# A new instruction order from batch 6 on, output passes exchanged, and the last store cut into quarters

## The chip, the core and the metric

The kernel runs on one core of a Trainium2 chip. Its five engines each take their own instructions in order and wait for one another by semaphores: TensorE (PE in the profile), VectorE (DVE), ScalarE (ACT), GpSimd (POOL) and SyncE (SP, which here only issues DMA transfers). The metric is device time in microseconds (us), lower is better.

## The reference

Two parts are chained. First an attention with pooled keys and values, for 8 batches, 8 heads, 576 positions of 64 channels, in fp32; then a feed-forward layer on the 4608 resulting rows.

```python
k_p = k.reshape(B, H, S // 8, 8, D).mean(axis=3)      # 72 pooled keys per head
v_p = v.reshape(B, H, S // 8, 8, D).mean(axis=3)
attn = softmax(q @ k_p.T / sqrt(D))
x = (attn @ v_p).transpose(0, 2, 1, 3).reshape(4608, 512)
h = x @ w_in                                          # 512 -> 2048
out = (h * sigmoid(1.702 * h)) @ w_out                # 2048 -> 512
```

## The kernel before

The result has to be exact to fp32 while the matmuls run in the fast fp32r mode, so each operand is split into a high and a low part and each product is three matmuls (high by high, high by low, low by high). From batch 2 on the products with w_in are combined by a scheme with seven block products for eight; for the last 512 rows ("late", called batch 7 here) w_out is treated the same way. Weight blocks in their combined form lie in DRAM and are fetched again for each batch.

The stretch that matters here, from about 650 us on, has four parts:

- Batch 6. For each of eight pairs p of feature tiles: products `ha6_p`, `hb6_p` (hidden units), activation, products `o6_*` (output, accumulated over the pairs in four PSUM banks). At its end ScalarE copies each `o` bank to an `osb` tile and issues its store at once (`finish`).
- The late hidden products (`hidden`): per pair seven products `la`, `lb`, `lc` of six 128x512 matmuls. Their operands are the combined weights `ws7_p` (three loads of 512 KB and one of 256 KB per pair, on SP's queue), their results are kept, added and passed through the activation by ScalarE and VectorE into tiles `store{p}_{th}`. PSUM banks are reused within a pair, so the next product waits for the copy of the last.
- Beside it `fold_out` combines the blocks of w_out: for each pair sums `u`, then high and low parts `tf{p}_0`, `tf{p}_1`, `tf{p}_2`, which SP stores to DRAM (`td{p}`) and later loads again (`ta{p}`, `tb{p}`). `tf{p}_2` takes its memory from the same two tiles as `osb`, so such a tile is free only when the store that reads it has landed.
- Two output passes (`outgoing`), th = 0 and th = 1, one per half of the late columns: for each of eight pairs seven products `m1` to `m7` of six 128x256 matmuls into seven PSUM banks, whose operands (`oa`, `ob`, `oc`, `od`, and sums `ou`) ScalarE, VectorE and GpSimd cut from `store`. At the end of a pass `combined` adds the seven banks into output tiles, which are stored: th = 0 goes to 512 rows in one piece (two transfers of 512 KB), th = 1 to the last 64 rows of each batch (four of 256 KB).

The order of all instructions is written out in the string `ORDER`, which a planner made beforehand; the kernel only reads it. A token is an engine and a task: `P:la7_4#1` is the second task of that name on TensorE; A is ScalarE, V VectorE, G GpSimd, D a transfer issued by SP, O a store of results. A star says that the task runs on its other engine, VectorE. Each engine gets its tasks in the order of the string. The costs that `plan.add` is given (0.7 for a store, say) were the planner's; when the kernel is built they have no effect. For `finish` the store is issued with the copy (`A:osb...`), and its `O` token emits nothing.

Of the kernel before, what the change touches and what calls it, by code (L numbers as in the profile page):

```python
# [14 lines left out]
ALU = mybir.AluOpType  # L15
# [3 lines left out]
P = 128  # L19
# [371 lines left out]
A:ah7_1#1 A:xtl0_0#3 V:al7_1#1 G:gl6_5#3 P:o6_128#10 *G:gl6_5#1 A:cs6_6#3 D:ws6_6#3 P:pav7_1#0 V:mt7_1#2 P:o6_384#10
P:o6_0#11 P:ha6_6#3 P:o6_128#11 A:xtl1_0#0 D:ws7_0#1 *A:ah7_1#2 P:pav7_1#1 A:yt1_0#0 A:cs6_6#4 A:gh6_6#1 P:ha6_7#0
V:cs6_6#1 A:gh6_6#0 P:hb6_6#2 P:o6_384#11 *A:y1_0#2 A:cs6_7#0 G:yt1_0#0 *A:xtl1_1#0 G:xtl0_1#0 *A:y1_1#2 V:al7_1#2
V:mt7_1#3 *A:xtl1_1#1 A:cs6_6#5 A:cs6_6#2 A:xtl1_0#1 P:ha6_7#1 P:o6_256#11 A:yt3_1#0 A:yt1_1#0 V:y1_1#2 A:cs6_7#1
V:cs6_6#2 *G:xtl1_0#0 A:gh6_6#3 V:y1_0#2 A:ah7_1#3 A:gh6_6#2 D:ws7_0#0 P:hb6_7#0 P:hb6_7#1 A:cs6_6#6 G:gl6_6#0
P:ha6_7#2 *G:gl6_6#1 G:yt1_1#0 V:al7_1#3 A:yt3_0#0 A:y2_1#0 P:pav7_1#3 *G:yt3_0#0 *A:y1_1#3 *G:yt3_1#0 A:cs6_7#3
P:pav7_1#2 A:cs6_6#7 A:xtl1_0#2 P:ha6_7#3 A:xtl1_1#3 P:o6_128#12 D:ws7_0#2 V:y1_1#3 A:y1_0#3 *G:y2_1#0 V:cs6_7#1
A:y2_0#0 D:ws7_1#0 V:y1_0#3 *G:gl6_6#3 V:cs6_7#0 *G:gl6_6#2 P:o6_0#12 A:xtl1_1#2 *G:xtl1_1#0 A:y2_1#1 *G:y2_0#0
P:o6_0#13 P:lb7_1#0 *G:xtl0_2#0 A:gh6_7#0 A:cs6_7#4 A:yt2_0#0 A:cs6_7#2 A:yt1_1#1 P:o6_384#12 P:hb6_7#2 *A:y2_0#1
*G:gl6_7#0 P:o6_256#12 G:xtl0_0#1 A:gh6_7#2 P:o6_128#13 A:yt4_1#0 P:o6_384#13 A:gh6_7#1 *G:y2_1#1 A:cs6_7#6  # L400
*G:gl6_7#2 D:ws7_1#3 *G:yt2_0#0 P:la7_0#0 P:o6_256#13 A:yt3_1#1 V:cs6_7#2 A:yt2_1#0 *G:y2_0#1 A:cs6_7#5 A:xtl1_0#3
*G:xtl1_1#1 A:gh6_7#3 P:la7_1#0 D:ws7_1#2 A:cs6_7#7 *G:yt2_1#0 A:yt4_0#0 G:yt4_1#0 *G:yt1_1#1 A:yt2_1#1 A:yt3_0#1
# [99 lines left out]
class Plan:  # L502
# [6 lines left out]
    def add(self, engine, us, emit, reads=(), writes=(), due=None, table=None, also=(), port=False, other=None, mode=None, lag=2.2):  # L509


        t = Task()
# [28 lines left out]
        for b in also:  # L541
            if b not in t.bufs:
                t.bufs.append(b)
                b.users += 1
# [31 lines left out]
def attention_moe_kernel(ctx: ExitStack, tc: tile.TileContext, q, k, v, w_in, w_out, out):  # L576


    nc = tc.nc
# [1910 lines left out]
```

## Time and profile before

| | us |
|---|---|
| median of 3 runs | 893.15 (892.63 to 893.85) |
| profiled execution | 894.48 |
| span of its profile, first to last instruction | 892.7 |
| TensorE busy | 872.2 |
| VectorE, ScalarE, GpSimd busy | 698.4, 538.0, 343.6 |
| mean granted TensorE clock | 0.992 |

The profiled execution has 1.8 us outside the span. Matmuls are pipelined and their ends are modelled, so TensorE counts as busy from the start of a matmul to the modelled end of the last; a gap in it is a wait, and its cost is read there and not from the share of the span.

### The profile page before, as it was taken

Reading aid. Unit: us, or ns where it says so; the run is one execution under the profiler, and the core shown is the slowest. Engines: PE = TensorE matmul, PEld = TensorE weight load, DVE = VectorE, ACT = ScalarE, POOL = GpSimd, SP = SyncE. Lnnn points to the kernel's source line nnn. Section 1 sums busy time; section 2 is a strip of 40 time slices with the busy share of each in tenths; the row PEclk is TensorE's granted clock in tenths of the full one; section 3 lists DMA queues with packets and bytes.
Section 4 is the critical chain, followed back from the end, with each engine's and each line's share of the span. In section 5 each row is a group of like instructions: output and inputs, shape, how many; then the busy total and the mean of one; then the engine's idle time right before and its main releaser. Section 6 shows DMA issues by size and latency. Waiting matters only on the chain.

```text
span 892.7 us, 15828 instructions
## 1 busy us (share of the span) xinstructions
PE 872.2 (98%) x5404; PEld 781.6 (88%) x5404; DVE 698.4 (78%) x1376; ACT 538.0 (60%) x1186; POOL 343.6 (38%) x345
## 2 busy tenths in 40 slices
PE   7999999999999999999999999999999999799997
PEld 6889898878899999998999989989998987589997
DVE  6998998779887876788878877889778756568885
ACT  4987655466556765767666665685657643247531
POOL 2768646666222124222521252236311226233322
PEclk9999999999999999999999999999999999899999
DMA  9972635646585768757884768567764448685011
GB/s 269 381 231 65 196 69 194 204 170 189 174 278 161 229 229 249 224 168 215 240 234 150 229 190 250 182 194 241 216 207 157 159 153 292 206 291 225 2 48 48
DMA packets 145792, 174.33 MB, mean 195 GB/s; under 512 B 85168, under 2 KB 96432, under 8 KB 145712
## 3 DMA queue, kind: packets, MB, share of 16 engines
q1 hardware_dynamic: 141392, 165.45, 59.4%
q10 hardware_dynamic: 4320, 7.87, 2.3%
q8 instruction: 43, 0.70, 0.3%
q14 instruction: 37, 0.30, 0.1%
HBM read 141.95 MB, written 31.33 MB: 194 GB/s over the span
## 4 chain that ended last, share of the span: by engine, by line
PE 87%; DMA 3%; DVE 3%; ACT 2%; SPq 1%; issue 1%; POOL 1%; DVEq 0%; POOLq 0%; ACTq 0%
PE ha L1881 13%; PE hb L1881 10%; PE m L2376 9%; PE o L2085 8%; PE o L2086 8%; PE o L2087 8%; PE sps L1127 4%; PE la L2154 3%; PE h L1676 3%; PE h L1677 3%; PE h L1678 3%; PE o L1718 2%; PE o L1719 2%; PE o L1720 2%; PE lc L2154 2%
## 5 line engine op out<-in xcount | busy, mean ns | idle before, releaser
L1935 POOL TENSOR_TENSOR glall<-shared,ghall 128x256 fp32r<-128x256 f32 x76 | 60.0, 794 | 203.4 <-ACT shared L1928 149.9
L2085 PE MATMUL o<-w,ghall 128*128 128x512 f32 x320 | 126.9, 397 | 0.0
L2086 PE MATMUL o<-w,ghall 128*128 128x512 f32 x320 | 126.2, 394 | 0.0
L2087 PE MATMUL o<-w,glall 128*128 128x512 f32 x320 | 125.0, 391 | 0.0
L2087 PEld LDWEIGHTS o<-w,glall 128*128 128x128 f32 x320 | 60.1, 188 | 13.8 <-POOL glall L1935 0.3
L1881 PE MATMUL ha<-xs,ws 128*128 128x256 f32 x480 | 71.1, 284 | 0.0
L1881 PEld LDWEIGHTS ha<-xs,ws 128*128 128x128 f32 x480 | 65.8, 190 | 4.8 <-ACT shared L1896 1.0
L1881 PE MATMUL hb<-x,ws 128*128 128x256 f32 x480 | 67.3, 283 | 0.0
L1881 PEld LDWEIGHTS hb<-x,ws 128*128 128x128 f32 x480 | 63.7, 190 | 3.0 <-DVE shared L1903 0.2
L2085 PEld LDWEIGHTS o<-w,ghall 128*128 128x128 f32 x320 | 60.6, 189 | 6.2
L2086 PEld LDWEIGHTS o<-w,ghall 128*128 128x128 f32 x320 | 60.7, 190 | 5.6
L1935 POOL TENSOR_TENSOR glall<-gall,ghall 128x256 fp32r<-128x256 f32 x42 | 32.4, 775 | 84.0 <-ACT gall L1928 51.8
L1676 PE MATMUL h<-x,w 128*128 128x256 f32 (+1 forms) x192 | 63.2, 329 | 1.3 <-ACT gh L1698 1.0
L1920 ACT ACTIVATE ghall<-shared 128x256 fp32r<-128x256 f32 x108 | 43.7, 415 | 33.9 <-DVE shared L1903 15.0
L1678 PE MATMUL h<-x,w 128*128 128x256 f32 (+1 forms) x192 | 61.1, 318 | 0.0
L1677 PE MATMUL h<-x,w 128*128 128x256 f32 (+1 forms) x192 | 61.1, 318 | 0.0
L1706 POOL TENSOR_TENSOR gl<-g,gh 128x512 fp32r<-128x512 f32 x28 | 40.0, 1427 | 47.6 <-ACT gh L1698 34.8
L1242 ACT COPY main<-sc 32x256 f32<-32x256 f32 (+2 forms) x109 | 49.6, 455 | 3.7 <-DVE sc L1199 1.9
L1903 DVE TENSOR_TENSOR shared<-shared,hb 128x256 f32<-128x256 f32 x81 | 33.4, 415 | 22.2 <-PE hb L1881 17.7
L1127 PE MATMUL sps<-k,qt 128*128 128x144 f32 x320 | 46.5, 290 | 1.7 <-ACT k L1034 0.7
L1127 PEld LDWEIGHTS sps<-k,qt 128*128 128x128 f32 x320 | 43.2, 191 | 4.1 <-ACT k L1034 1.1
L1928 ACT ACTIVATE shared<-shared 128x256 f32<-128x256 f32 x108 | 43.6, 414 | 3.1 <-ACT osb L1657 1.3
(264 smaller groups left out, 2446.9 us busy)
## 6 DMA issues: line engine op xcount, KB each, us to landing
ws<-wd SPq DMA_DIRECT2D x144, 512.0 KB
shared<-wd SPq DMA_DIRECT2D x48, 256.0 KB
wd<-stage SPq DMA_DIRECT2D x16, 512.0 KB
raw<-in_moe_w_in_dram SPq DMA_DIRECT2D x15, 512.0 KB
raw<-in_moe_w_out_dram SPq DMA_DIRECT2D x15, 512.0 KB
kv_False<-in_k_dram SPq DMA_DIRECT2D x28, 256.0 KB
kv_True<-in_v_dram SPq DMA_DIRECT2D x28, 256.0 KB
out_dram<-osb ACTq DMA_DIRECT2D x28, 256.0 KB
```

The costliest lines, as they stand in the source:

```text
L1127: nc.tensor.matmul(ps()[:, t * PW : (t + 1) * PW], lhsT=qt()[:, s0 : s0 + P], rhs=m.k2()[:, jj], start=True, stop=True,)
L1242: copy(out=main()[32 * r : 32 * (r + 1), :, cols].rearrange("p j t (k a) -> p t j a k", a=2), in_=sc()[rows, ts, :, 16 * r : 16 * (r + 1)] ...
L1676: nc.tensor.matmul(o, lhsT=w[:, 0, j], rhs=xs[:, 0], start=j == 0, stop=False)
L1677: nc.tensor.matmul(o, lhsT=w[:, 1, j], rhs=xs[:, 0], start=False, stop=False)
L1678: nc.tensor.matmul(o, lhsT=w[:, 0, j], rhs=xs[:, 1], start=False, stop=j == NJ - 1)
L1881: nc.tensor.matmul(o, lhsT=wv()[:, r, jj], rhs=xo(k, jj), start=start and n == 0, stop=n == len(terms) - 1,  skip_group_check=not start,)
L1935: engine.tensor_tensor(out=gl(), in0=part(i), in1=gh().bitcast(F32), op=ALU.subtract)
L2085: nc.tensor.matmul(o(), lhsT=gh()[:, tok], rhs=w()[:, 0], start=start, stop=False)
L2086: nc.tensor.matmul(o(), lhsT=gh()[:, tok], rhs=w()[:, 1], start=False, stop=False)
L2087: nc.tensor.matmul(o(), lhsT=gl()[:, tok], rhs=w()[:, 0], start=False, stop=stop)
L2154: nc.tensor.matmul(bank(), lhsT=wv()[:, r, jj], rhs=xs[jj]()[:, k], start=start and n == 0, stop=n == len(terms) - 1, skip_group_check=not ...
L2376: nc.tensor.matmul(bank()[:, i], lhsT=av(r)[:, i * P : (i + 1) * P], rhs=tv(k), start=p == 0 and i == n == 0, stop=p == NPAIR - 1 and n == ...
```

## The change

The first 3705 tokens of `ORDER` are the same, up to pair 2 of batch 6. From there on the order is new, and for many tasks the engine of the two that can do them. TensorE's work is the same matmuls. The two output passes are exchanged: th = 1 goes first, th = 0 last (`PASSES`), in the same PSUM banks by position. The last pair's products end in the order 1267543 for 1675432. Of the last pass each 256x256 quarter of the output (two row tiles by 256 columns) is stored by itself as it is done, and the quarter of the very last product `m3` is cut once more: its six matmuls become two tasks of three, each with its own VectorE addition and its own store of 128 rows by 256 columns, one issued by SP, one by ScalarE. `Buf` gets an argument `whole`, which holds a tile of which it is a part (it is used in making an order, and not when the kernel is built), and the stores have new costs.

Tasks by engine from the first token that differs, and from the first outgoing product on, counted in the two strings:

| | VectorE | ScalarE | GpSimd | tasks of TensorE |
|---|---|---|---|---|
| whole stretch, before | 342 | 247 | 81 | 265 |
| whole stretch, after | 369 | 232 | 70 | 266 |
| first outgoing product to end, before | 127 | 76 | 28 | 114 |
| first outgoing product to end, after | 155 | 71 | 25 | 123 |
| second pass alone, after | 67 | 20 | 10 | 57 |

Before, 151 tasks of TensorE stand ahead of the first outgoing product in the stretch, after it 143; nine `la`, `lc` products are mixed into the first pass.

```diff
@@ ORDER, around the last osb tile of batch 6 and pairs 2 to 4 of the late products
-D:ws7_4#2 D:td3_1#0 D:td3_0#0 D:td3_0#1 A:osb6_384#0 *A:store4_0#0 G:u4#1 *G:u4#2 *G:u4#3 A:w#37 *A:tf4_0#0
-V:store4_0#0 V:store3_1#0 P:la7_4#1 D:td2_0#0 D:ws7_5#1 *A:ob0_0#0 *G:tf4_1#0 O:osb6_384#0 G:w#37 A:tf4_2#0
-A:store4_1#0 P:lc7_3#1 A:store3_0#2 P:la7_4#2 *G:tf4_2#0 *G:ob0_0#0 D:ws7_4#3 G:u1_10#0 V:store3_1#1 P:la7_5#0
...
+A:store3_0#0 A:store0_1#2 V:store2_1#0 A:store1_0#1 V:store1_1#1 G:u2#0 P:la7_4#0 A:osb6_384#0 *G:u2#1 *G:u2#2
+A:tf2_0#0 D:ws7_4#1 P:lb7_3#0 P:lc7_2#1 A:store1_1#3 V:store3_0#0 *G:u2#3 D:td1_0#1 V:store2_1#1 A:store4_0#0
+P:la7_3#1 P:lb7_4#0 D:td2_0#0 D:ws7_4#2 *A:w#35 O:osb6_384#0 *G:tf2_1#0 A:store3_1#0 D:ws7_3#3 P:la7_3#2 P:lc7_3#0
+G:w#35 *A:tf2_2#0 P:la7_2#3 D:ws7_5#0 P:la7_4#1 G:tf2_2#0 A:store3_1#1 *G:u1_6#0 *G:u3#0 *G:u1_7#0 A:ob1_0#0
+D:td1_1#0 V:store4_0#0 D:td2_0#1 *G:u3#1 A:tf3_0#0 D:td2_1#0 V:store3_1#0 P:la7_3#3 *G:u3#2 P:lc7_3#1 *G:tf3_1#0
+A:store4_1#0 *G:u3#3 P:la7_4#2 *A:w#36 *G:w#36 A:tf3_2#0 G:tf3_2#0 G:u1_9#0 V:store3_1#1 *G:u1_8#0 D:ws7_6#0
+D:td3_0#1 *A:store4_1#1 P:lc7_4#0 D:ws7_4#3 D:ws7_5#1 D:ws7_5#3 G:u4#0 *G:u4#1 *A:store3_0#2 P:lb7_5#0 D:ws7_5#2
+P:la7_4#3 G:u4#2 V:store4_1#0 A:tf4_0#0 P:la7_5#0 D:td3_1#0 A:store4_0#1 D:ws7_6#1 *G:u4#3 *A:store4_0#2 D:td4_0#0
...
+G:tf6_2#0 A:oa1_1#0 *G:u1_14#0 *G:u7#0 D:ws7_7#3 P:la7_7#1 *G:u1_15#0 D:td6_0#0 A:store6_1#1 P:lb7_7#0 D:td5_1#0
+V:store6_1#0 D:td5_0#1 G:u7#1 *G:u7#2 D:td6_0#1 A:oa1_0#0 P:lc7_6#1 *A:store7_1#0 *A:tf7_2#0 G:u7#3 A:store6_1#2
@@ ORDER, the end
-P:m4_1#7 P:m5_1#7 V:store3_1#3 V:store3_1#2 P:m3_1#6 P:m3_1#7 V:store0_1#3 V:store2_1#2 O:store3_1#0 O:store2_1#0
...
+*G:ob0_7#0 *G:ob0_6#0 V:store0_0#1 V:store1_0#1 P:m5_0#7 V:store3_0#1 P:m4_0#6 O:store3_0#0 V:store0_0#2 P:m4_0#7
+P:m3_0#6 V:store3_0#2 O:store3_0#1 P:m3_0#7 V:store2_0#2 P:m3_0#8 V:store2_0#3 O:store2_0#1 O:store2_0#2
@@ outgoing
+    PASSES = (1, 0)
+    LAST_ORDER = "1267543"
+
+    def split_end(th, m):
+        return th == PASSES[-1] and m == LAST_ORDER[-1]
...
-        for m in "1675432" if p == NPAIR - 1 else "1245763":
+        for m in LAST_ORDER if p == NPAIR - 1 else "1245763":
             if p == 0:
-                bank_pool = BANKS[th][m]
+                bank_pool = BANKS[PASSES.index(th)][m]
...
-            pe(6 * 120, emit, [*a_refs, tb], [bank], mode="f32r")
+            if split_end(th, m) and p == NPAIR - 1:
+                for i in range(2):
+                    pe(3 * 120, lambda i=i, emit=emit: emit((i,)), [*a_refs, tb], [(bank, i)], mode="f32r")
+            else:
+                pe(6 * 120, lambda emit=emit: emit(range(2)), [*a_refs, tb], [bank], mode="f32r")
@@ combined
+        def cell(i, half, t):
+            return Part(osbs[i], (half, t), lambda v: v[:, t, 256 * half : 256 * half + 256])
...
+        def quadrant(i, half, x, m, op=ALU.add):
+            if split_end(th, m):
+                for t in range(2):
+                    dve(
+                        256,
+                        lambda t=t: nc.vector.tensor_tensor(
+                            out=cell(i, half, t)(), in0=cells(x)[:, t], in1=bank(m)()[:, t], op=op
+                        ),
+                        [(bank(m), t), ref(x)],
+                        [ref(cell(i, half, t))],
+                    )
+                    store_tile(i, half, t, cell(i, half, t))
+            else:
+                add(at(i, half), x, m, op)
+                if th == 0:
+                    store_quadrant(i, half, at(i, half))
+
         add(u2, a1, "6")
+        quadrant(0, 0, a1, "2")
         add(u3, u2, "7")
-        add(at(1, 1), u3, "5")
+        quadrant(1, 1, u3, "5")
         add(u2, u2, "5")
-        add(at(1, 0), u3, "4", ALU.subtract)
-        store_rows(th, 1, osbs[1])
-        add(at(0, 1), u2, "3")
-        add(at(0, 0), a1, "2")
-        store_rows(th, 0, osbs[0])
+        quadrant(1, 0, u3, "4", ALU.subtract)
+        quadrant(0, 1, u2, "3")
+        if th == 1:
+            for i in range(2):
+                store_rows(i, osbs[i])
...
-        plan.add("OUT", 0.7, emit, [osb])
...
+        plan.add("OUT", 1.9, emit, [osb])
+
+    def store_quadrant(i, half, part):
+        o0, d0 = LATE * S + i * HALF, 256 * half
+
+        def emit():
+            nc.sync.dma_start(
+                out=out[o0 : o0 + HALF, d0 : d0 + 256].rearrange("(t p) d -> p t d", p=P), in_=part()
+            )
+
+        plan.add("OUT", 1.0, emit, [ref(part)])
+
+    def store_tile(i, half, t, part):
+        o0, d0 = LATE * S + i * HALF + t * P, 256 * half
+        queue = (nc.sync, nc.scalar)[t]
+        plan.add(
+            "OUT", 0.5, lambda: queue.dma_start(out=out[o0 : o0 + P, d0 : d0 + 256], in_=part()), [ref(part)]
+        )
...
-    for th in range(2):
+    for th in PASSES:
```

## Rows read from the trace of the kernel before

**Rows 1.** The page, part 1: busy time, share of the span, instructions.

```profile
PE 872.2 (98%) x5404; PEld 781.6 (88%) x5404; DVE 698.4 (78%) x1376; ACT 538.0 (60%) x1186; POOL 343.6 (38%) x345
```

**Rows 2.** Waits of TensorE, 600 to 893 us: total, times, longest.

```profile
PE la L2154 <- ACT store L2166: 5.9, 1, 5.9
PE lc L2154 <- DVE store L2171: 0.5, 1, 0.5
```

**Rows 3.** Windows at the stall: busy PE, PEld, DVE, ACT, POOL; clock; DMA share; GB/s.

```profile
758.00:760.00 2.00, 2.00 (x11) 1.65 (x10) 1.64 (x4) 0.00 (x0) 0.14 (x1) 1.00 1.03 393
...
764.00:766.00 2.00, 0.00 (x0) 0.00 (x0) 0.00 (x0) 0.00 (x0) 0.00 (x0) 1.00 1.04 400
766.00:768.00 2.00, 0.00 (x0) 0.00 (x0) 0.00 (x0) 0.00 (x0) 0.00 (x0) 0.62 1.05 368
...
770.00:772.00 2.00, 2.00 (x6) 1.52 (x6) 1.91 (x3) 0.07 (x1) 1.03 (x2) 0.50 0.16 53
```

**Rows 4.** Timeline, 754 to 776 us: start, duration, engine, line, operation [idle before].

```profile
754.61 0.38 SPq L2259 DMA_DIRECT2D td<-tf  x1
...
760.49 0.59 ACT L1657 COPY osb<-o 128x512 f32<-128x512 f32 x1 [2.93 <-DMA td<-tf]
...
761.10 0.34 ACTq L1658 DMA_DIRECT2D out_dram<-osb  x1
...
768.69 0.40 ACT L2237 CAST tf<-u 128x256 fp32r<-128x256 f32 x1 [6.79 <-DMA out_dram<-osb]
...
769.63 2.93 PE L2154 MATMUL la<-yt,ws 128*128 128x512 f32 x6 [5.90 <-ACT store L2166]
...
772.36 1.99 PE L2154 MATMUL la<-y,ws 128*128 128x512 f32 x6
...
774.18 1.53 PE L2154 MATMUL lc<-yt,ws 128*128 128x512 f32 x6
...
775.56 1.52 PE L2154 MATMUL lb<-y,ws 128*128 128x512 f32 x6
```

**Rows 5.** Waits of ScalarE, 755 to 772 us.

```profile
ACT tf L2237 <- DMA out_dram<-osb: 6.8, 1, 6.8
ACT osb L1657 <- DMA td<-tf: 2.9, 1, 2.9
```

**Rows 6.** Timeline of the end, 882 us to the last instruction.

```profile
882.75 4.28 DVE L2409 TENSOR_TENSOR store<-store,m 128x512 f32<-128x512 f32 x6 [0.68 <-PE m L2376]
...
884.71 1.60 PE L2376 MATMUL m<-w,od 128*128 128x256 f32 x12
885.65 2.05 ACTq L2436 DMA_DIRECT2D out_dram<-store  x2
```

**Rows 7.** Windows of half a us at the end, columns as in rows 3.

```profile
886.50:887.00 0.50, 0.00 (x0) 0.00 (x0) 0.50 (x1) 0.00 (x0) 0.00 (x0) 1.00 0.00 0
887.00:887.50 0.50, 0.00 (x0) 0.00 (x0) 0.03 (x1) 0.00 (x0) 0.00 (x0) 1.00 0.89 205
...
889.50:890.00 0.50, 0.00 (x0) 0.00 (x0) 0.00 (x0) 0.00 (x0) 0.00 (x0) 0.50 1.06 393
...
890.50:891.00 0.50, 0.00 (x0) 0.00 (x0) 0.00 (x0) 0.00 (x0) 0.00 (x0) 0.50 0.32 119
```

**Rows 8.** The page, part 5: groups of instructions by line.

```profile
L1903 DVE TENSOR_TENSOR shared<-shared,hb 128x256 f32<-128x256 f32 x81 | 33.4, 415 | 22.2 <-PE hb L1881 17.7
```

**Rows 9.** One window from the first outgoing product to the last.

```profile
803.00:886.40 83.40, 83.31 (x684) 82.59 (x682) 66.22 (x125) 38.18 (x74) 26.19 (x26) 1.00 0.20 75
```

**Rows 10.** DMA view, 735 to 800 us.

```profile
DMA packets 6746, 17.03 MB, mean 262 GB/s; under 512 B 746, under 2 KB 746, under 8 KB 6743
```

**Rows 11.** Timeline, 875 to 878 us, GpSimd and VectorE.

```profile
875.14 1.74 POOL L2325 TENSOR_TENSOR oc<-ou,oc 128x512 fp32r<-128x512 f32 x1
...
875.65 1.52 DVE L2325 TENSOR_TENSOR ob<-store,ob 128x256 fp32r<-128x256 f32 x1
...
877.43 0.41 DVE L2325 TENSOR_TENSOR ob<-store,ob 128x256 fp32r<-128x256 f32 x1
```

More of the change, by code (lines that the diff above doesn't have):

```diff
@@ L416 @@
-P:la7_3#2 D:ws7_5#0 *G:u1_9#0 D:td2_0#1 A:store3_1#1 D:ws7_4#1 P:la7_4#0 *G:u1_8#0 P:lc7_3#0 *G:u4#0 P:la7_3#3
-D:ws7_4#2 D:td3_1#0 D:td3_0#0 D:td3_0#1 A:osb6_384#0 *A:store4_0#0 G:u4#1 *G:u4#2 *G:u4#3 A:w#37 *A:tf4_0#0
-V:store4_0#0 V:store3_1#0 P:la7_4#1 D:td2_0#0 D:ws7_5#1 *A:ob0_0#0 *G:tf4_1#0 O:osb6_384#0 G:w#37 A:tf4_2#0
-A:store4_1#0 P:lc7_3#1 A:store3_0#2 P:la7_4#2 *G:tf4_2#0 *G:ob0_0#0 D:ws7_4#3 G:u1_10#0 V:store3_1#1 P:la7_5#0
-P:lc7_4#0 D:td1_1#0 *G:u1_11#0 *G:u5#0 A:store4_1#1 G:u5#1 D:td4_0#0 P:lb7_5#0 D:ws7_5#2 *A:store5_0#0 *G:u5#2
@@ new lines @@
+A:tf2_0#0 D:ws7_4#1 P:lb7_3#0 P:lc7_2#1 A:store1_1#3 V:store3_0#0 *G:u2#3 D:td1_0#1 V:store2_1#1 A:store4_0#0
+P:la7_3#1 P:lb7_4#0 D:td2_0#0 D:ws7_4#2 *A:w#35 O:osb6_384#0 *G:tf2_1#0 A:store3_1#0 D:ws7_3#3 P:la7_3#2 P:lc7_3#0
+G:w#35 *A:tf2_2#0 P:la7_2#3 D:ws7_5#0 P:la7_4#1 G:tf2_2#0 A:store3_1#1 *G:u1_6#0 *G:u3#0 *G:u1_7#0 A:ob1_0#0
+D:td1_1#0 V:store4_0#0 D:td2_0#1 *G:u3#1 A:tf3_0#0 D:td2_1#0 V:store3_1#0 P:la7_3#3 *G:u3#2 P:lc7_3#1 *G:tf3_1#0
+A:store4_1#0 *G:u3#3 P:la7_4#2 *A:w#36 *G:w#36 A:tf3_2#0 G:tf3_2#0 G:u1_9#0 V:store3_1#1 *G:u1_8#0 D:ws7_6#0
@@ new lines @@
+D:td3_0#1 *A:store4_1#1 P:lc7_4#0 D:ws7_4#3 D:ws7_5#1 D:ws7_5#3 G:u4#0 *G:u4#1 *A:store3_0#2 P:lb7_5#0 D:ws7_5#2
+P:la7_4#3 G:u4#2 V:store4_1#0 A:tf4_0#0 P:la7_5#0 D:td3_1#0 A:store4_0#1 D:ws7_6#1 *G:u4#3 *A:store4_0#2 D:td4_0#0
+A:store2_1#2 D:td3_0#0 A:tf4_2#0 *G:tf4_2#0 G:tf4_1#0 P:lc7_4#1 G:ob1_0#0 D:td4_1#0 *A:w#37 A:store5_0#0 G:w#37
+V:store2_0#0 G:u1_11#0 *G:u1_10#0 A:store0_0#3 P:la7_5#1 A:store3_1#2 V:store4_1#1 G:u5#0 D:ws7_7#0 *G:u5#1
+P:lc7_5#0 A:store5_1#0 A:tf5_0#0 *G:u5#2 G:u5#3 A:store1_1#2 P:la7_5#2 *A:tf5_2#0 V:store5_0#0 *A:store5_1#1 *A:w#38
@@ L540, in add @@
                 (b.writes if is_write else b.reads).append((t, key))
-        for b in also:
+        for b in (*also, *(b.whole for b in t.bufs if b.whole is not None)):
             if b not in t.bufs:
@@ L723, in share @@
         ring = slots.setdefault(i, Ring(1, fifo=True))
-        return Buf(ring, lambda: whole()[:, i], name), whole
+        return Buf(ring, lambda: whole()[:, i], name, whole), whole
     def hold(t, *bufs):
@@ L1837, in g_slot @@
         state[0] += 1
-        return Buf(ring, view, f"{what}{nm}"), whole
+        return Buf(ring, view, f"{what}{nm}", whole), whole
     c_slots = []
@@ L1853, in c_slot @@
         c_slots[0] += 1
-        return Buf(ring, view, f"cs{nm}"), whole
+        return Buf(ring, view, f"cs{nm}", whole), whole
     def pair(c, p, due, then):
@@ new lines, in combined, with store_rows @@
+        quadrant(0, 1, u2, "3")
+        if th == 1:
+            for i in range(2):
+                store_rows(i, osbs[i])
+    rows = out.rearrange("(b s) d -> b s d", s=S)
+    def store_rows(i, osb):
+        def emit():
+            for e, queue in enumerate((nc.sync, nc.scalar)):
+                queue.dma_start(
+                    out=rows[4 * i + e : 4 * i + 4 : 2, CHUNK:].rearrange("t s d -> s t d"),
+                    in_=osb()[e * LEFT : (e + 1) * LEFT],
+                )
+        plan.add("OUT", 1.9, emit, [osb])
```

202 lines of the change are left out of this document (94 added, 108 removed).

## Prediction

> **What bounds the kernel now.** I read the page first: TensorE is busy for 98% of the span [rows 1], so a change to this kernel can only win where TensorE stands still, where its clock is low, or behind its last matmul. The table of waits of TensorE over the last third, the part that the new order rewrites, has two entries: one wait of 5.9 us for ScalarE, one of 0.5 us for VectorE [rows 2]. It lists no other gap there. The windows around the long wait [rows 3] show what it costs beside the idle time: the granted clock is 1.00 until 766 us and 0.50 in 770 to 772, the lower of the two levels (1.2 of 2.4 GHz).
>
> The timeline says what happened [rows 4]. ScalarE copies the last output tile of batch 6 into an osb tile at 760.49 and issues its store at 761.10. ScalarE's next cast, tf4_2, needs an osb tile again, and there are two. It starts at 768.69, 6.8 us late, and the wait is put down to that store [rows 5]. So the store took 7.6 us from issue to release (761.10 to 768.69). Behind the cast on ScalarE's queue stands the PSUM copy that the next la product waits for; TensorE stands for 5.90 us, from 763.73 to 769.63 [rows 4]. The osb copy itself had waited 2.9 us for a td store that was issued at 754.61, 5.9 us before [rows 4, 5], and TensorE did not stop for that one: about 3 us of such lateness is covered.
>
> The third place is the end: TensorE's last matmul ends at 886.31 (884.71 + 1.60), VectorE's last addition at 887.03, the span at 892.7 [rows 6]. So 6.4 us lie behind the last matmul.
>
> **The change, part by part.** *The stall.* In the old order one la product stands between the osb6_384 copy and tf4_2, which takes the tile that this copy's store frees. A product is 1.38 us (774.18 to 775.56 [rows 4]), so tf4_2 asked 1.4 us after the copy for something that took 7.6. In the new order osb6_384 comes before pair 2's sums, and six products stand before the next user of its tile, tf2_2 (now on VectorE): 8.3 us, more than 7.6. Of the other users of osb tiles up to pair 6 the nearest stand three products (4.1 us) behind the store they wait for. Against the two landings seen (5.9 and 7.6 us) that leaves waits of 1.8 to 3.5 us, near the 2.9 us that cost nothing. So I take the stall away whole: 5.90 us of idle time, and the slow clock. The twelve matmuls from 769.63 to 774.18 took 4.55 us where two products take 2.76: 1.8 us. Together 7.7 us. The 0.5 us wait stands in the same stretch and may go or stay; I leave it in the sum and give it to the lower bound.
>
> *The passes change places.* What was stored last were four transfers, 1.05 MB, all issued from 885.65 on; bytes flow from 887.0 (nothing before, 205 GB/s after) to about 890.7, and 2.0 us later the span ends [rows 6, 7]. In the new order these four go out inside the second pass. Two of them are issued by SP, which has nothing else left, and two by ScalarE (2.05 us for its pair at 885.65, a wait included [rows 6]), where 20 operations remain in a pass of 56 products, 41 us (six matmuls each, 684 in 83.4 us [rows 9]); so I cost it at nothing. Without that cover it would be at most these 2.05 us.
>
> *The end in quarters.* The last store now is 131 KB per queue. From TensorE's end: VectorE adds 128x256 from PSUM in 0.41 us [rows 8]; issue to first byte 1.35 us (885.65 to 887.0 [rows 6, 7]); 131 KB at 393 GB/s 0.35 us [rows 7]; then 2.0 us to the end. That is 4.1 us against 6.4: at best 2.3 us gained. The other bound: both halves of the last product lie in one PSUM bank, and if the second half's matmuls wait until VectorE has read the first, that adds 0.45 us (its read, and the second half behind it) and a restart of at most the 0.5 that the short wait cost [rows 2]; if the 1 KB rows move at half the rate, 0.35 more; and VectorE already runs its last six additions without a break (4.28 us [rows 6]), so it may come 0.2 late. Then 0.8 us are gained. Nothing in the trace shows a split bank; I take 1.5, the middle.
>
> *Engines set anew.* Between the first outgoing product and the end VectorE gets 155 operations for 127, ScalarE 71 for 76, GpSimd 25 for 28. VectorE was busy 66.2 us of 83.4 with 125 operations, 0.53 us each [rows 9]. The stretch now starts eight products earlier: 83.4 + 11.0 = 94.4 us, and 155 x 0.53 = 82 us. VectorE goes from 79% to 87%; TensorE still covers it, so I cost it at nothing. If that cover goes, VectorE's work sets the end of the passes (third rival).
>
> *What costs nothing.* The stores' new costs and the `whole` of Buf emit no instruction; they act through the order alone. In batch 6 and in pairs 0 and 1 the order changes too, and TensorE has no wait there now. The nearest thing to one in the new order: a load of ws6_4 (third block) stands on SP behind one of ws6_5 that waits for TensorE to release its place, which leaves ten tasks until its use, 6.6 us (most of three 128x512 matmuls, half a la product or 0.69); the stores above landed in 5.9 to 7.6 us in the busiest stretch, so at most 1.0 us, which is in the first rival.
>
> The sum: 7.7 + 1.5 = 9.2 us off the profiled span, 892.7 to 883.5; that execution took 894.48 in all, 1.8 outside the span, and the median of the runs is 893.15. Taken off the median: **884.0 us**. With all small gains (0.5 for the other wait, 2.3 for the end) it is 10.5, so 882.6; the lowest of the runs shown lies 0.5 under their median, so 882.1 as the low end.
>
> **Rivals.** *A new wait in the same stretch (28 in 100).* The SP queue runs in order. In the new order the load of ws7_4's last quarter stands behind the store td3_0 (low half), which needs a VectorE operation, tf3_1; from that operation's place to the product that uses the load there are three products, 4.1 us, less 0.7 for the operation (six took 4.28 us in [rows 6]): 3.4 us. If the load lands as the stores did, after 5.9 to 7.6 us, TensorE stands 2.5 to 4.2 us, and 1.8 more if the clock falls again: 886.5 to 890.0. A second such place is tf7_2 on VectorE, one product behind td5_1, with the first pass's operands queued behind it. Against it: SP and VectorE run ahead of their places where they are free. Such a wait covers the range's upper end.
>
> *The transfers are the bound there, and the stall stays (7 in 100).* Around the stall the DMA engines are busy all the time (1.03 to 1.05, 368 to 400 GB/s [rows 3]). If that, and not the place of the store, makes ScalarE late, only the end's 1.5 us come: 891.6. Against it: over 735 to 800 us they move 262 GB/s in the mean [rows 10], two thirds of the 400, and no wait of TensorE names a load. The Trainium skill ("DMA: Bandwidth & Descriptors", Issuing engines are not separate DMA queues) says that transfers issued from different engines run on the same 16 DMA engines and interleave. By that rule the store from ScalarE gains nothing from its own queue, and the trace agrees: it took 7.6 us beside SP's loads.
>
> *VectorE becomes the bound, and the kernel is slower (5 in 100).* The place is the two outgoing passes. An addition of 128x256 by VectorE took 1.52 us at 875.65 while GpSimd's operation of 875.14 to 876.88 ran, and 0.41 at 877.43 [rows 11]. The mechanism would be that VectorE's operations with two SBUF inputs wait for GpSimd's. It decides when the mean goes over 94.4 / 155 = 0.61 us, and eats the gain of 9.2 at 0.67. If each of the 28 added operations took the 1.1 us more: 82 + 31 = 113 us, 18.6 over TensorE's, and 884.0 + 18.6 = 902.6. The Trainium skill ("SBUF — State Buffer", SBUF: two separate sides) states this as an exclusive lock: whichever of a VectorE operation with two SBUF inputs and a GpSimd operation starts first holds the shared port pair for its whole length. By that rule moving additions from GpSimd to VectorE costs nothing where GpSimd rests, and the 1.52 us agrees with it. Against the rival: GpSimd has fewer operations here than before, and the 0.53 already holds such waits.
>
> **How the numbers follow.** The forecast has 60 in 100, with 882.1 to 885.2 as its own range (the bounds of the end, the wait of 0.5, the spread of the runs). The new wait has 28, with 886.5 to 890.0. The range 882.1 to 890.0 holds both, nominally 88; I leave it so since the new order may hold a place I did not see. A measurement of this kernel tells about 0.2% (1.8 us) from no change. Below 891.4 lie the forecast and the new wait, 88; the second rival at 891.6 and the small change of a worse new wait are "same", 6; slower are VectorE's case and a rest, 6.
>
> **What would show it.** Right: no wait of TensorE over 2 us behind 650 us, a granted clock of 1.00 from there to the last matmul, waits of ScalarE or VectorE for stores of at most 3.5 us; at the end, less than 5.6 us between last matmul and end of span, with less than 0.5 MB moving behind it. Wrong: a wait of la, lb or lc for a load or for a store buffer; m products waiting for VectorE; a mean VectorE operation over 0.6 us in the passes; or an end as long as before, because the last product's two halves take turns with VectorE.

## The result, and the profile after

| us | before | after |
|---|---|---|
| median (lowest to highest of 4 runs) | 893.02 (892.63 to 893.85) | 882.37 (881.54 to 884.38) |
| span of the profiled execution | 892.7 | 879.7 |
| mean granted clock | 0.992 | 0.999 |

The ratio is 0.9883, with a 95% interval of 0.9865 to 0.9901: faster by 1.2%, 10.6 us. The forecast was 884.0: the kernel came out 1.6 us below it, and the low end of the range, 882.1, is only just kept.

The waits of TensorE from 600 us to the end, total, times, longest, answer to [rows 2]:

```profile
PE m L2383 <- DVE store L2433: 0.5, 1, 0.5
```

The waits for ScalarE and VectorE in the late products are gone; a new one stands in the last product. Windows at the time of the old stall (columns as in [rows 3]) show a full TensorE and a clock of 1.00, while the DMA engines are about as busy as they were (a share of 0.85 in the window at 766, of 1.00 to 1.07 in the five others from 760 to 772):

```profile
760.00:762.00 2.00, 2.00 (x10) 1.68 (x9) 0.91 (x2) 0.00 (x0) 1.36 (x2) 1.00 1.06 394
...
764.00:766.00 2.00, 2.00 (x11) 1.65 (x10) 2.00 (x3) 1.70 (x4) 2.00 (x3) 1.00 1.07 340
...
770.00:772.00 2.00, 2.00 (x10) 1.65 (x9) 0.78 (x2) 0.94 (x2) 1.15 (x2) 1.00 1.02 342
```

The timeline of the changed kernel around the last `osb` copy answers to [rows 4]:

```profile
747.67 0.57 ACT L1658 COPY osb<-o 128x512 f32<-128x512 f32 x1
748.27 0.34 ACTq L1659 DMA_DIRECT2D out_dram<-osb  x1
...
751.60 0.38 SPq L2260 DMA_DIRECT2D td<-tf  x1
751.63 0.83 DVE L2238 CAST tf<-u 128x256 fp32r<-128x256 f32 x1
```

The copy of `osb6_384` is at 747.67, its store at 748.27, and the cast that needs an `osb` tile next, `tf2_2`, begins on VectorE at 751.63 without a wait. The other tile was still held then, since its store `td1_1` goes out only at 751.60. So the store of the copy freed its tile within 3.4 us, where the store in [rows 4] took 7.6.

The end, as in [rows 6], and in windows of half a us, as in [rows 7]:

```profile
874.15 1.24 PE L2383 MATMUL m<-w,od 128*128 128x256 f32 x9
875.42 0.42 DVE L2433 TENSOR_TENSOR store<-store,m 128x256 f32<-128x256 f32 x1 [0.39 <-PE m L2383]
875.87 0.34 SPq L2482 DMA_DIRECT2D out_dram<-store  x1
...
875.90 0.62 PE L2383 MATMUL m<-w,od 128*128 128x256 f32 x3 [0.51 <-DVE store L2433]
876.56 0.42 DVE L2433 TENSOR_TENSOR store<-store,m 128x256 f32<-128x256 f32 x1 [0.71 <-PE m L2383]
877.01 0.35 ACTq L2482 DMA_DIRECT2D out_dram<-store  x1
```

```profile
876.50:877.00 0.50, 0.02 (x1) 0.00 (x0) 0.42 (x1) 0.00 (x0) 0.00 (x0) 1.00 0.87 303
877.00:877.50 0.50, 0.00 (x0) 0.00 (x0) 0.00 (x0) 0.00 (x0) 0.00 (x0) 1.00 0.27 90
877.50:878.00 0.50, 0.00 (x0) 0.00 (x0) 0.00 (x0) 0.00 (x0) 0.00 (x0) 0.75 0.20 72
878.00:878.50 0.50, 0.00 (x0) 0.00 (x0) 0.00 (x0) 0.00 (x0) 0.00 (x0) 0.50 0.55 191
878.50:879.00 0.50, 0.00 (x0) 0.00 (x0) 0.00 (x0) 0.00 (x0) 0.00 (x0) 0.50 0.00 0
```

Three matmuls of the last product end at 875.39 (the group of nine at 874.15 holds six of the product before). The other three start at 875.90, after VectorE's addition of the first half. From the last matmul's end, 876.52, to the end of the span, 879.7, lie 3.2 us, for 6.4 before.

**Two stretches that repeat.** The token order is the same up to batch 6, so both kernels run the same `hb` product at about 596 us:

```profile
597.11 0.87 PE L1881 MATMUL hb<-xs,ws 128*128 128x256 f32 x6
```

```profile
595.73 0.86 PE L1882 MATMUL hb<-xs,ws 128*128 128x256 f32 x6
```

From its start to the start of the last twelve matmuls (874.15 here, 884.71 in [rows 6]) is the first stretch, from there to the end of the span the second. In the profiled executions of kernels that share the new order these agree within 0.1 us, while medians of one kernel moved by 0.3 us (the changed one) to 1.7 us (the one before), so the experiments below are read by them. The kernel before and a1 have one profile each; that their first stretches repeat as well is not shown.

| kernel | first stretch | second stretch | span | median |
|---|---|---|---|---|
| before | 287.60 | 7.99 | 892.7 | 893.02 |
| after | 278.42 | 5.55 | 879.7 | 882.37 |
| a0: after, again | 278.39 | 5.59 | 881.0 | 882.69 |
| a1: before, one store earlier | 280.44 | 8.00 | 888.7 | 886.71 |
| a2: after, last copy late | 283.78 | 5.59 | 886.0 | 887.65 |
| a3: after, GpSimd rests | 279.73 | 5.58 | 881.8 | 883.32 |
| b0: after, last product whole | 278.37 | 5.36 | 879.6 | 882.29 |
| b1: b0, whole tiles at the end | 278.37 | 5.98 | 880.9 | 883.19 |
| b2: after, two banks | 278.40 | 4.85 | 880.8 | 882.55 |
| b3: after, a load later | 282.78 | 5.53 | 884.8 | 885.76 |
| c0: b1, stores of 64 partitions | 278.45 | 7.73 | 883.8 | 886.41 |
| c1: b1, stores on two queues | 278.46 | 5.84 | 882.0 | 883.42 |

The kernel before had medians of 894.71 beside a0 to a3, 893.6 beside b0 to b3 and 893.99 beside c0 and c1; each ratio below is against its own.

The change took 9.2 us from the first stretch and 2.4 from the second, 11.6 in all. The two spans differ by 13.0; the other 1.4 lie ahead of 596 us, where the code is the same. That part moves from run to run: the `hb` product begins at 595.73 in the changed kernel's first profile, at 597.02 in its second, and at 600.26 in a1, whose profiled execution (890.35) was the slowest of its six.

### The profile page after: what moved, and what is told of

Its sections match the earlier page's. It is cut to its first block, busy times and chain, and to the rows that moved or that the text cites. A ratio compares the mean times of both kernels' runs of the same rounds, so it can differ in the third digit from the quotient of the medians.

```text
span 879.7 us, 15816 instructions
## 1 busy us (share of the span) xinstructions
PE 868.7 (99%) x5404; PEld 780.0 (89%) x5404; DVE 709.1 (81%) x1403; ACT 531.0 (60%) x1171; POOL 333.7 (38%) x334
## 4 chain that ended last, share of the span: by engine, by line
PE 94%; ACT 2%; DVE 1%; SPq 1%; DMA 1%; issue 1%; POOL 0%; ACTq 0%; POOLq 0%; DVEq 0%
PE ha L1882 13%; PE hb L1882 10%; PE m L2383 9%; PE o L2086 8%; PE o L2087 8%; PE o L2088 8%; PE la L2155 5%; PE sps L1128 4%; PE h L1677 3%; PE h L1678 3%; PE h L1679 3%; PE o L1719 3%; PE o L1720 3%; PE o L1721 3%; PE lc L2155 2%; PE lb L2155 1%
## 5 line engine op out<-in xcount | busy, mean ns | idle before, releaser
L1936 POOL TENSOR_TENSOR glall<-gall,ghall 128x256 fp32r<-128x256 f32 x46 | 35.3, 771 | 95.2 <-ACT gall L1929 62.2
```

What stands on the lines that cost most here:

```text
L1936: engine.tensor_tensor(out=gl(), in0=part(i), in1=gh().bitcast(F32), op=ALU.subtract)
```

## The experiments

**The changed kernel again (a0)**, as a control for a1 to a3, which ran on the same chip.

> The changed kernel as it is, beside the others of this group. It took 882.4 us (881.5 to 884.4), 10.6 less than before. If that holds here, 881 to 884. The first 594 us are the same instructions in both kernels, but the changed one's profile was 1.4 us ahead there; I expect that part to be no more than 0.7 ahead in the mean, so the change itself to bring 9 to 11.

882.69 (882.37 to 882.86), ratio 0.9864, 0.9841 to 0.9886, and the same single wait. The time is as expected; the difference to the kernel before, 12.0 us, lies over the expected 9 to 11, since that kernel's median was 1.7 us higher here than in the first runs.

**One store earlier in the old order (a1).** `tf1_2` holds one of the two `osb` tiles until its store `td1_1` has landed. In the old order that store stands behind `tf4_2`, so `tf2_2`, `tf3_2`, `osb6_384` and `tf4_2` all go through the other tile; the waits in [rows 5] agree for the last two. Only this token is moved:

```diff
 ... D:td1_0#0
+D:td1_1#0
 G:u1_6#0 G:u3#0 P:lc7_2#0 ... A:osb6_384#0 ... A:tf4_2#0 ... P:lc7_4#0
-D:td1_1#0
```

> The kernel before with one token moved: the store td1_1 is issued right behind td1_0's first half, not fifteen products later. So tf1_2's tile is free early, and tf4_2 does not have to take the tile of the osb6_384 store. Theory (the stall is that one shared tile): ScalarE's wait of 6.8 us at tf4_2 falls under 3, TensorE's wait of 5.9 us and the half clock behind it go, 893.0 - 7.7 = 885.3 us (884.3 to 886.5). Rival (the transfers are the bound there): the wait moves to another task, time within 2 us of 893.

886.71 (885.57 to 890.35), ratio 0.9913, 0.9891 to 0.9935. The waits of TensorE in it, 600 us to the end:

```profile
PE lb L2141 <- DMA ws<-wd: 0.6, 1, 0.6
PE lc L2141 <- DVE store L2158: 0.5, 1, 0.5
```

The median lies 0.2 us over the expected range, beside a kernel before that was 1.7 us slower here. The wait of 5.9 us is gone, and with it the low clock. That `tf4_2` now has the other tile is seen in the timeline: ScalarE casts it at 764.06, 2.1 us behind the issue of the `osb6_384` store, whose bytes move from 763.1 to 765.7.

```profile
761.98 0.34 ACTq L1645 DMA_DIRECT2D out_dram<-osb  x1
...
764.06 0.40 ACT L2224 CAST tf<-u 128x256 fp32r<-128x256 f32 x1
```

The first stretch is 7.2 us shorter than before although a wait of `lb` for a load came in. So one transfer, moved by itself, gives over three quarters of what the whole new order gives there.

**The last copy late in the new order (a2).** The copy `osb6_384` goes directly ahead of the cast `tf2_2`, six products of TensorE later in the string; its `O` token, which emits nothing, goes with it.

```diff
-A:osb6_384#0
 *G:u2#1 ... P:lc7_3#0 G:w#35
+A:osb6_384#0 O:osb6_384#0
 *A:tf2_2#0
```

> The changed kernel with one token moved: the osb6_384 copy, and with it its store, stands right before tf2_2, which takes the same tile, instead of six products ahead. Theory: VectorE waits 5.5 to 7.5 us at tf2_2, TensorE then stands 3 to 6 us for a sum or copy of VectorE, with up to 1.8 us of half clock: 4 to 7.7 us over the changed kernel, 886.5 to 890. Rival (the gain comes from the engines set anew): less than 1 us over it.

887.65 (885.64 to 890.1), ratio 0.9919, 0.9896 to 0.9942, and a first stretch 5.4 us longer. Waits of TensorE, then the timeline of it:

```profile
PE lc L2142 <- DVE store L2159: 3.8, 1, 3.8
PE m L2370 <- DVE store L2420: 0.5, 1, 0.5
```

```profile
752.44 0.38 SPq L2247 DMA_DIRECT2D td<-tf  x1
...
753.55 0.34 ACTq L1646 DMA_DIRECT2D out_dram<-osb  x1
...
759.88 0.29 DVE L2225 CAST tf<-u 128x256 fp32r<-128x256 f32 x1 [7.31 <-DMA td<-tf]
...
764.35 2.21 PEld L2142 LDWEIGHTS lc<-y,ws 128*128 128x128 f32 x6 [4.21 <-DVE store L2159]
```

The copy's store is issued at 753.55, `tf2_2` starts at 759.88, `lc` stands for 3.79 us and its six matmuls then take 2.93 us. But the cast's wait is put down to the store issued at 752.44, which is `td1_1`, and not to the copy's store. That is right: bytes of the copy's store, the only transfer of ScalarE there, still move when the cast has begun (7 packets, 0.01 MB, from 759.9 to 760.5). So `tf2_2` took the tile that `tf1_2` had held, 7.4 us behind the issue of `td1_1`, and not, as was expected, the tile of `osb6_384`. With the copy this late neither tile is free in time: `td1_1` holds one, the copy and its store the other. A stall of the old kind is back in the new order, with the wait at the other tile.

**GpSimd rests in the passes (a3).** All 25 tasks of GpSimd from the first outgoing product on go to VectorE (a star before each), as:

```diff
-G:ou1_1#0 ... G:od0_7#0
+*G:ou1_1#0 ... *G:od0_7#0
```

> The changed kernel with all 25 tasks that GpSimd has from the first outgoing product on given to VectorE, which then has 180 operations there. At 0.53 us each that is 95 us against 94 of TensorE; without GpSimd beside it an operation should take nearer 0.49, 88 us. Theory (VectorE is covered): within 1.5 us of the changed kernel, no wait of an m product over 1 us. Rival (VectorE is at its bound): 3 us over it or more, with m products that wait for VectorE.

883.32 (882.9 to 886.3), ratio 0.9877, 0.9855 to 0.9899. Its waits of TensorE, and one window over the passes, with the changed kernel's behind it (columns as in [rows 9]):

```profile
PE m L2370 <- DVE oa L2313: 1.1, 1, 1.1
PE m L2370 <- DVE store L2420: 0.5, 1, 0.5
```

```profile
792.00:875.00 83.00, 81.92 (x664) 80.89 (x664) 72.75 (x161) 31.92 (x60) 0.00 (x0) 1.00 0.29 99
```

```profile
792.00:874.15 82.15, 82.15 (x672) 81.47 (x671) 69.86 (x141) 31.27 (x58) 23.57 (x20) 1.00 0.29 98
```

VectorE does 161 operations in 72.75 us, 0.45 each, where it did 141 in 69.86, 0.50 each, beside GpSimd. So the added 20 cost it 2.9 us of work, where 20 at the 0.41 us of [rows 11] would be 8.2: its other operations took some 5 us less without GpSimd beside them. By shapes the same is seen: an addition `ou<-store,ou` took 0.584 us beside GpSimd and 0.421 without it, a cast `ob` 0.467 and 0.291. TensorE lost 1.1 us in one wait, where none over 1 us was expected.

**The last product whole (b0).** The tokens of the second halves go too.

```diff
-        return th == PASSES[-1] and m == LAST_ORDER[-1]
+        return False
```

> The changed kernel, its last product not cut: one task of six matmuls, one addition of 128x512, one store of 256 KB by SP. Theory (the halves take turns with VectorE in one PSUM bank, so the cut gives back what it gains): counted from the end of the product's third matmul, the changed kernel needs 4.3 us to the end of its span; uncut it is 0.6 (second half) + 0.7 (addition) + 3.1 (a store that took 2.7, and 0.35 for the second 131 KB) = 4.4 us. No wait of TensorE at the end, and a time within 0.5 us of the changed kernel's 882.5: 882.0 to 883.0. Rival (the cut is what shortened the end): 1 us or more longer, 883.5 to 884.5.

882.29 (881.42 to 884.6), ratio 0.9872, 0.9854 to 0.989; no wait of TensorE behind 600 us. The second stretch is 5.36 us, for 5.55 with the cut: cutting the last product costs 0.2 us here.

**Whole tiles at the end (b1).** From b0, the tiles of the last pass, th = 0, are stored as those of th = 0 were before the change, in two transfers of 512 KB by SP.

```diff
-                if th == 0:
-                    store_quadrant(i, half, at(i, half))
...
-        if th == 1:
-            for i in range(2):
-                store_rows(i, osbs[i])
+        for i in range(2):
+            (store_rows if th == 1 else store_half)(i, osbs[i])
```

> The changed kernel, its last pass not stored by quarters: the last product is whole, and the two output tiles of th = 0 go out in two transfers of 512 KB, each when its tile is done, as before the change; the exchanged passes and the new order stay. Theory (the end got shorter since only a small part of the output moves behind the last matmul): 1.05 MB moves again behind it, about 2.7 us at 393 GB/s from 0.8 us behind the last matmul, then 1.3 to 2.0 us: 4.8 to 5.5 us from the last matmul to the end, for 3.2, and TensorE's wait of 0.5 is gone: 1.1 to 1.8 us over the changed kernel, 883.6 to 884.3. Rival (the order of the passes alone made the end short): within 0.4 us of the changed kernel, 882.1 to 882.9.

883.19 (882.68 to 885.95), ratio 0.9885, 0.9866 to 0.9903. The second stretch is 5.98 us, between both expectations: 0.6 us longer than by quarters, but 2.0 shorter than before, although the same 1.05 MB moves behind the last matmul. So most of what the end gained did not come from the quarters. What differs from the old end is how the bytes are cut into transfers; the next two tell this apart.

**Stores of 64 partitions (c0), and on two queues (c1).** From b1; c0 has the shape of the old end's transfers with the rows of th = 0.

```diff
-            nc.sync.dma_start(out=out[o0 : o0 + HALF].rearrange("(t p) d -> p t d", p=P), in_=osb())
+            rows_i = out[o0 : o0 + HALF].rearrange("(t p) d -> p t d", p=P)
+            for e, queue in enumerate((nc.sync, nc.scalar)):
+                queue.dma_start(out=rows_i[e * LEFT : (e + 1) * LEFT], in_=osb()[e * LEFT : (e + 1) * LEFT])
```

`LEFT` is 64. In c1 the last line is

```diff
+                queue.dma_start(out=rows_i[:, e], in_=osb()[:, e])
```

> The kernel with whole tiles at the end, each tile of th = 0 stored in two transfers of 256 KB, one by SP with the lower 64 partitions of the tile, one by ScalarE with the upper 64, as the tiles of th = 1 were at the end before the change; the rows that they go to are th = 0's, all in a piece. With two transfers of 128 partitions by SP, 4.74 us lie between the end of the last product's third matmul and the end of the span; before the change it was 6.75. Theory (a transfer from 64 partitions moves at about half the rate and starts later): 6.3 to 6.9 us, nothing moves until 1.3 us behind the first issue, then some 200 GB/s: 1.6 to 2.1 us over that kernel, 884.8 to 885.3. Rival (two queues, or the scattered rows of th = 1, made the old end long; the partitions don't matter): 4.5 to 5.2 us, 882.9 to 883.7.

> The kernel with whole tiles at the end, each tile of th = 0 stored in two transfers of 256 KB over all 128 partitions, one by SP, one by ScalarE. Theory (the partitions decide, not the queues): 4.5 to 5.0 us from the end of the last product's third matmul to the end of the span, some 400 GB/s, a time of 882.9 to 883.5. Rival (transfers of two queues at the same time get in each other's way): 6.0 us or more and 200 GB/s while both run, 884.5 to 885.3.

c0: 886.41 (885.57 to 888.11), ratio 0.9922, 0.9901 to 0.9943; second stretch 7.73, 6.5 us from the end of the third matmul. c1: 883.42 (881.61 to 884.59), ratio 0.988, 0.986 to 0.99; 5.84 and 4.6. Timeline and windows of c0, then of c1:

```profile
876.07 1.60 PE L2369 MATMUL m<-w,od 128*128 128x256 f32 x12
876.99 2.07 ACTq L2457 DMA_DIRECT2D out_dram<-store  x2
877.02 2.00 SPq L2457 DMA_DIRECT2D out_dram<-store  x2
```

```profile
877.50:878.00 0.50, 0.17 (x2) 0.00 (x0) 0.29 (x1) 0.00 (x0) 0.00 (x0) 1.00 0.00 0
878.00:878.50 0.50, 0.00 (x0) 0.00 (x0) 0.40 (x1) 0.00 (x0) 0.00 (x0) 1.00 0.48 115
878.50:879.00 0.50, 0.00 (x0) 0.00 (x0) 0.00 (x0) 0.00 (x0) 0.00 (x0) 1.00 0.93 201
879.00:879.50 0.50, 0.00 (x0) 0.00 (x0) 0.00 (x0) 0.00 (x0) 0.00 (x0) 1.00 0.98 168
```

```profile
876.16 1.60 PE L2369 MATMUL m<-w,od 128*128 128x256 f32 x12
877.08 1.81 ACTq L2457 DMA_DIRECT2D out_dram<-store  x2
```

```profile
877.50:878.00 0.50, 0.26 (x3) 0.05 (x1) 0.20 (x1) 0.00 (x0) 0.00 (x0) 1.00 0.07 29
878.00:878.50 0.50, 0.00 (x0) 0.00 (x0) 0.48 (x1) 0.00 (x0) 0.00 (x0) 1.00 1.04 406
878.50:879.00 0.50, 0.00 (x0) 0.00 (x0) 0.00 (x0) 0.00 (x0) 0.00 (x0) 1.00 1.08 422
```

c0's median lies 1.1 us over the expected 885.3, its end of 6.5 us inside the expected 6.3 to 6.9; c1 came as its theory said.

Both issue at the same place behind the last product, and both move 576 packets. In c1 bytes move at 406 to 422 GB/s from 0.9 us behind the issue; in c0 nothing moves until 1.2 us behind it, and then 168 to 201 GB/s at a DMA share of 0.93 to 0.98, like the old end's 205 in [rows 7]. In these 1.5 us all of c0's packets are of the queue that carries ScalarE's stores (q10 in the DMA view; in b1, where SP issues alone, it moves nothing): the two stores, issued 0.03 us apart, go one after the other. Later the rate rises, to 340 at 880.0 in c0 as to 393 in [rows 7]. The 1.05 MB take 4.3 us in c0 (878.2 to 882.5) and 2.9 us in c1 (877.9 to 880.8). So 64 partitions, not two queues and not the scattered rows, made the old end long: 1.75 us of b1's 2.0; for the rest no run was made. The Trainium skill ("DMA: Bandwidth & Descriptors", Rules for kernel authors) says that two transfers to disjoint halves of the partitions serialize, since they share the same engines, and advises one over 128. The runs agree: the first two stores of c0 go one after the other, and its second stretch is 7.73 us against b1's 5.98.

**Two banks for the last product (b2).** Each half of it gets a PSUM bank of its own (`V:store3_1#3` and the first two products of `m3` in the last pass change place for it).

```diff
+                count = 2 if split_end(th, m) else 1
+                acc[th, m] = [
+                    buf(bank_pool, [P, 2, 256], F32, bank_pool.name[-1], f"m{m}_{th}") for _ in range(count)
+                ]
...
-                            bank()[:, i],
+                            banks[i]()[:, 0] if len(banks) > 1 else banks[0]()[:, i],
```

> The changed kernel, the two halves of the last product in two PSUM banks, so that VectorE's reading of the first half holds nothing up; to free the bank one addition is taken earlier, and the first two products of m3 in the last pass start after the first of m6. Theory: the wait of 0.5 us between the halves goes, and the end comes 0.5 to 0.75 us earlier: 881.8 to 882.0 where the changed kernel has 882.5. Rival (the wait is no matter of the bank, but of the release that VectorE signals, or VectorE is late itself): the wait stays or VectorE's last addition is no earlier: 882.3 to 882.7. If the moved addition makes TensorE wait elsewhere, that shows as an m product waiting for VectorE.

882.55 (881.07 to 884.26), ratio 0.9872, 0.9852 to 0.9892. TensorE has no wait behind 600 us, and the second stretch is 4.85 us, 0.7 shorter:

```profile
875.95 1.60 PE L2373 MATMUL m<-w,od 128*128 128x256 f32 x12
877.23 0.78 DVE L2423 TENSOR_TENSOR store<-store,m 128x256 f32<-128x256 f32 x2 [0.39 <-PE m L2373]
```

The twelve matmuls run through, and VectorE's two additions follow each other. By the stretches it is the best kernel of all, 0.7 us ahead of the changed one. The medians can't tell 0.7 us (0.08%) from no change: 882.55 lies where the rival was put, and only the trace speaks for the theory, since the wait is gone and the last addition is earlier.

**A load later (b3).** `D:ws7_4#3` goes behind three other loads on SP's queue, to the issue time that the prediction's first rival feared.

```diff
-D:ws7_4#3
 D:ws7_5#1 D:ws7_5#3 ... P:lb7_5#0 D:ws7_5#2
+D:ws7_4#3
 P:la7_4#3
```

> The changed kernel, with the load of the last quarter of ws7_4 moved behind three other loads on SP's queue. In the changed kernel it is issued at 758.0 and its product begins at 764.97, 7.0 us later, with no wait. Here it would be issued at about 761.4, 3.5 us ahead, about the 3.4 us of the prediction's first rival. Theory (the rival's price was right, and it did not come since VectorE and SP ran ahead of their places): a load needs 5.9 to 7.6 us there, so a product la stops for ws for 2.4 to 4.1 us, up to 1.8 more by the clock: 884.9 to 888.4. Rival (a load lands within 3.5 us, the price was wrong as well): no wait of TensorE over 1 us, 882.2 to 883.2.

885.76 (884.18 to 886.63), ratio 0.9905, 0.9889 to 0.992; first stretch 4.4 us longer.

```profile
762.17 0.42 SPq L1801 DMA_DIRECT2D shared<-wd  x1
...
768.39 2.44 PE L2142 MATMUL la<-yt,shared 128*128 128x512 f32 x6 [2.54 <-DMA shared<-wd]
...
770.63 2.34 PE L2142 MATMUL la<-y,ws 128*128 128x512 f32 x6
```

Issued at 762.17, used at 768.39: 6.2 us, a wait of 2.5 for TensorE, and two products in 4.4 us (768.39 to 772.81) where they take 2.7. In the changed kernel the same load goes out 3.4 us earlier, counted from the `hb` product (595.73 there, 596.49 here):

```profile
756.89 0.68 DVE L2241 TENSOR_TENSOR tf<-u,tf 128x512 fp32r<-128x512 f32 x1
...
757.60 0.32 SPq L2254 DMA_DIRECT2D td<-tf  x1
...
758.01 0.40 SPq L1814 DMA_DIRECT2D shared<-wd  x1
...
764.97 1.52 PE L2155 MATMUL la<-yt,shared 128*128 128x512 f32 x6
```

VectorE runs `tf3_1` at 756.89, which lets the store `td3_0` and then the load out at 758.01, 7.0 us ahead of its product at 764.97.

## Why the prediction was right, step by step

**The stall: right, in size too.** 7.7 us were costed; a1, which takes away that wait and little else, shortens the first stretch by 7.2 and brings in a wait of 0.6. a2 shows from the other side that the place of the copy counts: with the copy late a stall comes back, though at the other tile. Three things behind it were off. The prediction gave the new order six products, 8.3 us, between the copy and the tile's next user; in time it was 4.0 (747.67 to 751.63), and it was enough since the store took at most 3.4 us there. It named the spacing but not why one tile had to do for all: the late store `td1_1` kept the other. (It does so in the new order too, until after 751.60; there it is the spacing at the one free tile that works.) And it took the landings seen, 5.9 and 7.6 us, for those of the whole stretch, where they depend on what SP has in flight. The DMA view tells ScalarE's queue (q10) from SP's (q1) by packets, MB and packet time as a share of 16 engines; first the kernel before from 764.00 to 768.50, then the changed one from 749.00 to 750.60:

```profile
q1 hardware_dynamic: 560, 1.46, 87.9%
q10 hardware_dynamic: 144, 0.26, 15.1%
```

```profile
q10 hardware_dynamic: 144, 0.26, 42.4%
q1 hardware_dynamic: 110, 0.21, 33.3%
```

From the issue of the copy's store to its first byte lie 3.0 us before, in which SP's queue moves 0.70 MB, and 0.8 us in the changed kernel, with 0.26 MB; in a1 it is 1.1 us and 0.46 MB, in a2 3.9 us and 0.95 MB. That SP's transfers make the store late is argued from these four; no run changes them alone.

**The other wait: under-counted.** The first stretch gained 9.2 us, 1.5 more than the stall's 7.7. Over the whole stretch TensorE is busy for 281.11 of 287.60 us before and for all of the 278.42 after. So 6.5 us were idle time (5.9, 0.5 and 0.1), and its matmuls took 2.7 us longer, of which the slow clock is the 1.8 that was costed. The second entry of [rows 2], left as 0.5 in the lower bound, belongs to the gain; the 0.9 us of longer matmuls that are left no row places.

**The end: right in kind, wrong in two terms.** 1.5 us were taken, 2.4 came (7.99 to 5.55 in the second stretch), a little over the upper bound of 2.3. The step that gave the last store 1.35 us to its first byte, 0.35 for its bytes and 2.0 to the end failed: the store issued at 877.01 is done at 879.7, 2.7 us and not 3.7, of which 0.8 lie ahead of the first byte (877.8), 0.6 are its bytes (until 878.4) and 1.3 lie behind them. The first term was read off transfers from 64 partitions, which start later (1.2 us in c0, 0.9 in c1). The last was read too long, since bytes of the old end move until 891.0, 1.7 us from the end; why that is more than the 1.3 here and in c0 stays open. "The passes change places" was costed at nothing, but it is what took those transfers away from the end: b1 puts 2.0 of the 2.4 there, the quarters add 0.6, and the cut takes 0.2 back. The feared turn-taking in one bank did come: a wait of 0.51 us, and b2, which removes it, gains 0.7. The Trainium skill ("PSUM — Partial Sum Buffer", PSUM bank collisions raise a hardware error) asks for PSUM to be guarded by bank, or by bank and quadrant, and not by address; the kernel behaves so, since the second half's matmuls, in columns of their own, wait for the addition.

**Engines set anew: right.** VectorE is at 85% in the passes (69.86 of 82.15 us) for the 87% forecast, 0.50 us an operation for 0.53. The rival that VectorE becomes the bound did not come near its 0.61, and a3 shows why: work moved away from GpSimd gives part of its price back.

**The rivals.** The new wait at `ws7_4` was priced rightly and did not occur: b3 measures 2.5 us and 1.7 of slow clock at a lead that the prediction had estimated for the changed kernel. The lead was 7.0 us there, since VectorE and SP ran ahead of their places. `tf7_2` made no wait. Transfers as the bound fell: the DMA engines are about as busy as before in those windows and TensorE does not wait; that SP's transfers made the store of [rows 4] late is likely all the same, as the queues above show. (This rival has 7 in 100 where it is told and 6, with another case, in the last sum.) Of what was to show it right, all is there: no wait over 0.5 us, a clock of 1.00, one wait for a store, ScalarE's 1.3 us ahead of 727.62, where 3.5 were allowed, and 0.33 MB behind the last matmul (0.5 us each at 303, 90, 72 and 191 GB/s from 876.5).

**The number.** 7.7 + 1.5 = 9.2 us off, where the stretches show 11.6. Taken as the prediction did from the median, 893.15 − 11.6 = 881.5; the measured 882.37 lies 0.9 above that, less than the 1.3 by which the start of the `hb` product moved between the changed kernel's two profiles. That the time lies inside the range was thus in part luck: by the stretches alone it would have come out 0.6 us under the low end.

## What to carry to other kernels

When an engine waits for a buffer of a pool of two, look for the buffer that is not in the row: a transfer issued late can hold it, so that the pool works as one, and moving that one transfer can be worth most of a new order. The place in an instruction string says little of the time, and nothing certain of the buffer that an instruction gets (a2); leads of loads and buffers are read in us between issue and use, and price and occurrence of a wait are two questions. At the end of a kernel, store from all 128 partitions, and count its tail from a transfer of the same shape.

## What the runs showed of the hardware

- Two stores from the two halves of the partitions, issued together (c0), went one after the other at first, at 168 to 201 GB/s and a DMA share above 0.9; the same bytes over 128 partitions (c1) began at 406 to 422. All 1.05 MB took 4.3 us against 2.9.
- A store of 256 KB from ScalarE freed its tile within 3.4 us when issued at 748.27, took 7.6 at 761.10 (before), and still moved bytes 6.4 us after its issue at 753.55 (a2). One landing time for a stage is too coarse.
- VectorE's 161 operations without GpSimd took 72.75 us, hardly more than 141 beside it (69.86).
